# Loading q, k and v of an attention kernel into 128-partition tiles with longer rows

## The chip, the cores and the metric

The kernel runs on one core of a Trainium2 chip. The metric is the device time of one execution in microseconds. The core has five engines that the text names: TensorE (PE in the profile, its weight loads are PEld), VectorE (DVE), ScalarE (ACT), GpSimd (POOL) and SyncE (SP, which here issues all DMA transfers).

## The reference

The input has 4 batches, 8 heads, 576 tokens and head size 64. First a double attention: 32 learned rows p attend to k and v, and then q attends to the packed result. Two mixture-of-experts layers follow. Cut to the attention part:

```python
def sm_attn(qq, kk, vv):
    s = scale * np.matmul(qq, kk.transpose(0, 1, 3, 2))
    s = s - np.max(s, axis=-1, keepdims=True)
    a = np.exp(s)
    a = a / (np.sum(a, axis=-1, keepdims=True) + 1e-09)
    return np.matmul(a, vv)
p_packed = sm_attn(p, k, v)
out = sm_attn(q, p_packed, p_packed)
```

The output, as 2304 tokens of 512 features, goes through a first layer of 8 experts (each token to the expert with the largest logit, up to a capacity), and through a second with an output gate. Tensors are float32.

## The kernel before

**Attention.** A batch is worked in two halves G of four heads. Each half of k, q and v is one transfer into a tile "r" of 96 partitions: a partition holds, for each of the four heads, six tokens in sequence, 1536 contiguous bytes. `transp` turns k and q by TensorE transposes of [96, 128] into T (head size on partitions, the tokens' parity u in the upper and lower 64), and ScalarE evicts them from PSUM. `s1_mm` makes the first scores (p with k; the 32 rows p of four heads on 128 partitions), `s1_max` and `s1_exp` the first weights a1, `a1_T` transposes a1 back to tokens on partitions, and `pp_mm` multiplies by v. `pp_scale` and `pp_T` give the packed rows ppT.

The second softmax has only 32 columns. `s2_mm` makes its scores (q with ppT), `s2_tr` transposes them on VectorE in blocks of 32 by 32 into sT, where max, subtraction, exp, sum and product run over the 32 (the subtraction and the product on GpSimd), and `s2_back` transposes them back into a2T, whose columns are the tokens in order. For that, q's columns in T must have a certain order; the eviction of q writes them so, with a stride of three elements:

```python
if nm == "q":
    o = o.rearrange("x u (p j) -> x u j p", j=J)
    i = i.rearrange("x u (j p) -> x u j p", j=J)
```

**Order.** It is written out by hand. `att_iter(b)` does the first scores of batch b, the rest of batch b - 1, and the second softmax of batch b - 2, and transposes k of batch b + 1. Loads are issued on SP's queue ahead of each iteration: k of batch b + 2, then q's first half, v, and q's second half of batch b + 1. `att_last` does the last scores and the routing of batch 0, and `att_end` the rest, with pieces of the first expert layer filled in between. Logits of the gates (`g1_l`, from a2T) choose the experts whose weights SP then loads, so their place in time sets when the expert layers can start.

**Experts.** The weights are split into two float32r parts (`split`), and each product is made of three matmul passes. From the end of the attention on, TensorE runs the four expert layers nearly without a gap.

Of the kernel before, what the change touches and what calls it, by code (L numbers as in the profile page):

```python
# [28 lines left out]
def tile_kernel(  # L29
# [21 lines left out]
    KP = 96  # L51
    R = S // KP
    J = R // 2
    HS = S // 2
    NT = -(-S // 128)
# [44 lines left out]
    zt = const.tile([KP, 128], FP32, name="zt")  # L100
# [54 lines left out]
    # ================= gating: pieces =================  # L155
# [3 lines left out]
    def onehot(L, nm, V=nc.vector):  # L159
        """of the logits L [128,n,E]: bf16 one-hot of the first largest, and L less its largest; in two pieces"""  # L160
# [17 lines left out]
    def denom(ex, nm):  # L178
        """1 / (softmax sum + 1e-9)"""
        nc.scalar.activation(out=ex, in_=ex, func=ACTF.Exp)  # L180
        den = sm_p.tile([128, ex.shape[1]], FP32, tag=nm + "den", name="den")
        nc.vector.tensor_reduce(den, ex, axis=AX.X, op=ALU.add)
        nc.vector.tensor_scalar(den, den, 1e-9, None, op0=ALU.add)
        nc.vector.reciprocal(den, den)
        return den

    def counts(K16, dst):
        """dst [1,n,E] = kept tokens of each of n batches per expert"""
# [9 lines left out]
    def primary(c, nm, pe, mu, ne, V=nc.vector):  # L198
        """of the counts c [1,n,E]: the index of the largest, more than one?, any?"""
# [22 lines left out]
    # ================= attention =================  # L222
    att, att_r = ExitStack(), ExitStack()
    apool = pool_in(att)
    qkv_p = apool("qkv", 9)
# [24 lines left out]
    def load(b, nm, gs=(0, 1)):  # L250
        src = {"k": k, "q": q, "v": v}[nm]
        for G in gs:
            t = qkv_p.tile([KP, 4, R, D], FP32, tag="r", name="r")
            nc.sync.dma_start(t, src[b, 4 * G:4 * G + 4].rearrange("h (p r) d -> p h r d", r=R))
            raws[nm, b, G] = t

    def transp(b, nm, G, eng=0):
        """[96, 4 heads, row, d] -> [128 (row parity, d), 4 heads, 288]"""
        src = raws.pop((nm, b, G))
        t = t_p.tile([128, 4, HS], FP32, tag="T", name="T")  # L260
        for hh in range(2):
            ps = psm("tp")
            for u in range(2):
                for j in range(J):
                    tr(nc, ps[:, u, j * KP:(j + 1) * KP], src[:, 2 * hh + u, 2 * j:2 * j + 2, :].rearrange("p r d -> p (r d)"),
                       ident[:KP, :KP])
            i = ps[:, :, 0:HS]
            o = t[:, 2 * hh:2 * hh + 2, :]
            if nm == "q":
                o = o.rearrange("x u (p j) -> x u j p", j=J)  # L270
                i = i.rearrange("x u (j p) -> x u j p", j=J)
            evac(eng, o, i)
        T[nm, b, G] = t
# [9 lines left out]
    def score(lhs, rhs):  # L283
        """lhs(u, hq) [64,32], rhs [128, 4, 288] -> psum [128 (hq, pack), u, 288]"""
        s = psm("s")
        for hq in range(4):
            for u in range(2):
                mm(nc, s[32 * hq:32 * hq + 32, u, 0:HS], lhs(u, hq), rhs[64 * u:64 * u + 64, hq, :], True, True)
        return s
# [10 lines left out]
    def s1_exp(b, G):  # L300
        a1 = at_p.tile([128, 2, HS], FP32, tag="a1", name="a1")
        if G == 0:
            at["sm", b] = as_p.tile([128, 2], FP32, tag="sm", name="sm")
        nc.scalar.activation(out=a1, in_=at.pop(("s1", b, G))[:, :, 0:HS], func=ACTF.Exp,
# [8 lines left out]
    def a1_T(b, G, eng=0):  # L313
        a1 = at.pop(("a1", b, G))
        ps = psm("a1Tp")
        for u in range(2):
            for j in range(J):
                tr(nc, ps[:KP, u, j * 128:(j + 1) * 128], a1[:, u, j * KP:(j + 1) * KP], ident)
        t = at_p.tile([KP, 2, J, 128], FP32, tag="a1T", name="a1T")
        evac(eng, t, ps[:KP, :, 0:J * 128].rearrange("p u (j n) -> p u j n", j=J))  # L320
        at["a1T", b, G] = t

    def pp_mm(b, G):
        if G == 0:
            at["pp", b] = psm("pp")
        pp, t, vt = at["pp", b], at.pop(("a1T", b, G)), raws.pop(("v", b, G))
        for u in range(2):
            for j in range(J):
                for hq in range(4):
                    mm(nc, pp[32 * hq:32 * hq + 32, G, 0:D], t[:, u, j, 32 * hq:32 * hq + 32],  # L330
                       vt[:, hq, 2 * j + u, :], u == 0 and j == 0, u == 1 and j == J - 1)
# [52 lines left out]
    def s2_back(b, G):  # L384
        nc.vector.transpose(a2T[:, b, G].rearrange("p (n i u) -> p u n i", i=32, u=2), at.pop(("sT", b, G)))

# [11 lines left out]
    def g1_l(b0, b1):  # L398
        """logits' parts on partitions 32 (2 u + G) + E * place: of head group G, tokens 256 u .. 256 u + LW"""
# [29 lines left out]
    def gb(b0, b1):  # L429
        """rank of each token among the earlier ones of its expert"""  # L430
# [35 lines left out]
    # ================= experts =================  # L466
# [6 lines left out]
    def split(src, nm, i, lo_eng):  # L473
        """piece i of a weight matrix: two float32r parts that add up to it"""
# [12 lines left out]
    def new_h(last_first=False):  # L487
        """[128, chunk, token], high and low parts; last_first: the low parts of the last tile's tokens come first"""
# [3 lines left out]
    def moe1_load1(e):  # L492
        """the raw pieces of w1, rows split by head group: [128 (G, d), hq, f]"""
# [30 lines left out]
    def ppw_mm(pt, w):  # L524
        """(a2 pp) w1 = a2 (pp w1): pp w1 of 256 columns"""
# [15 lines left out]
    def chain(ps, seq, mid={}):  # L541
        """ps [128, 2, HS] = sum of stationary.T @ moving over seq; mid: other work, by the step it goes before"""
# [6 lines left out]
    def layer1(h, f, w, x, n, last_first=False):  # L549
        """h[f] = relu(w.T x), split; w, x: (hi, lo)"""  # L550
# [13 lines left out]
    def moe1_layer2(h, ws, c, y, mid={}):  # L564
        """y[c] = w2.T h, split"""
# [12 lines left out]
    def g2_l(y):  # L578
        """logits of both gates: rows from the high part of the gates, rows from the low part"""
# [28 lines left out]
    def g2_g(oel, g1s, slot):  # L608
        """the gates of the second experts, times those of the first"""
# [32 lines left out]
    def moe2_layer2(h, ws, t, g2, bsel):  # L642
        """rows of token tile t: (h.T w2) times the gates"""
# [62 lines left out]
    # ================= what the two slots leave =================  # L706
    def more(dst):
        """dst [1,1] = the number of batches and slots whose tokens go to more than one expert"""
# [4 lines left out]
    def slot(i, slots_i):  # L713
        """both expert layers of one more batch"""
# [24 lines left out]
    def general():  # L739
        """every expert over the tokens it is given, whatever the routing"""  # L740
# [25 lines left out]
        def mask(K):  # L766
            """msk [128, BT] = tokens of the loop's expert"""
# [5 lines left out]
        def masked(dst, src, b):  # L773
            """dst = src [128, n, S] where the expert's tokens are, else 0"""
# [76 lines left out]
    # ================= the program =================  # L851
# [5 lines left out]
    with tc.manual_schedule():  # L857
# [8 lines left out]
        def att_iter(b):  # L866
            """scores and weights 1 of batch b, the rest of batch b - 1, softmax 2 and logits of batch b - 2"""
# [46 lines left out]
        def att_last():  # L914
            """the last scores 1, with the gating of batch 0 between them"""
# [41 lines left out]
        def att_end():  # L957
            """the rest of the last batch"""
# [73 lines left out]
        # first expert layer of slot 0, between the pieces of the last batch  # L1032
# [82 lines left out]
        for i in (2, 3):  # L1115
            bz = val(slots_i[0:1, 0, i - 1:i], B - 1)
            nc.sync.dma_start(
                out.rearrange("(b p r) (x d) -> b p (r x) d", b=B, r=R, d=128)[bass.ds(bz, 1)].rearrange(
                    "o p r d -> p (o r) d"),
                zt.unsqueeze(1).to_broadcast([KP, S * DM // (KP * 128), 128]))  # L1120
# [90 lines left out]
```

## Time and profile before

| | us |
|---|---|
| median of 3 runs | 290.41 (287.1 to 293.39) |
| profiled execution: span from first to last instruction | 289.3 |
| TensorE busy | 259.8 (90%) |
| VectorE busy | 131.1 (45%) |
| ScalarE busy | 105.4 (36%) |
| GpSimd busy | 44.6 (15%) |
| DMA | 37.16 MB, 128 GB/s on average |

Of the profiled execution's own time the profile gives the span; it is 1.1 us below the median. Busy shares are means over stages with different limits, so the stages have to be looked at one by one. A row of a timeline or of a group names line, engine, operation, output tile, input tiles and the shape, partitions by elements; "[3.75 <-DMA r]" is idle time of the engine ahead of the instruction and what ended it. The DMA share is that of 16 engines, as a fraction; values a little above 1 occur where packets overlap.

### The profile page before, as it was taken

The page shows a single profiled execution, that of the slowest core. Times are in us where ns is not written, and L with a number is a line of the kernel's source. Part 1 is how long each engine was busy: PE and PEld are TensorE (multiplying, and loading weights), DVE is VectorE, ACT ScalarE, POOL GpSimd, SP SyncE. Part 2 cuts the span into 40 slices and gives each one's busy share as a digit, 9 for nine tenths or more (in the row PEclk, how much of TensorE's full clock was granted, in tenths as well). Part 3 has the DMA queues.
Part 4 walks back from the last instruction along what each step waited for, and adds up shares of the span by engine and source line. Part 5 has one row for each costly group of instructions (what it writes and reads, how often), then busy time and mean ns, then how long its engine had stood idle before and what let it go on. Part 6 is the DMA issues. An engine that isn't in the chain of part 4 may idle for free. (4 is left out here: it accounts for less than half of the span.)

```text
span 289.3 us, 5848 instructions
## 1 busy us (share of the span) xinstructions
PE 259.8 (90%) x2401; PEld 226.1 (78%) x2401; DVE 131.1 (45%) x316; ACT 105.4 (36%) x160; POOL 44.6 (15%) x69
## 2 busy tenths in 40 slices
PE   7785949969699898999979999999999999999990
PEld 5565739546479877997879999999888899998870
DVE  0230543858779948617972133359422053640000
ACT  2583537466435412125641224116232143431000
POOL 5000113315415206000533000000010000000100
PEclk9996975998889999999979999999999999999997
DMA  7999999990794000299378622502701181000111
GB/s 176 234 245 199 220 230 239 237 230 9 173 254 160 0 2 0 98 215 227 98 210 227 228 75 72 147 0 76 217 36 54 39 268 61 2 0 36 59 39 44
DMA packets 33828, 37.16 MB, mean 128 GB/s; under 512 B 4224, under 2 KB 30464, under 8 KB 33792
## 3 DMA queue, kind: packets, MB, share of 16 engines
q1 hardware_dynamic: 33792, 36.69, 50.2%
q8 instruction: 21, 0.34, 0.5%
q14 instruction: 15, 0.12, 0.1%
HBM read 31.25 MB, written 4.72 MB: 124 GB/s over the span
## 5 line engine op out<-in xcount | busy, mean ns | idle before, releaser
L21 PE MATMUL o<-w2bh,h 128*128 128x512 f32 x144 | 45.9, 391 | 0.0
L21 PE MATMUL y<-h,w2ah 128*128 128x288 f32 x256 | 44.6, 296 | 0.0
L21 PEld LDWEIGHTS y<-h,w2ah 128*128 128x128 f32 x256 | 37.6, 189 | 0.0
L562 DVE SCALAR_TENSOR_TENSOR h<-h 128x576 fp32r<-128x576 f32 (+3 forms) x64 | 25.8, 446 | 23.6 <-ACT h L555 23.6
L555 ACT ACTIVATE h<-h 128x576 fp32r<-128x576 f32 x32 | 20.4, 650 | 35.0 <-PE h L21 31.2
L25 PE MATMUL tp<-ident,r 96*128 96x96 f32 x192 | 24.1, 290 | 10.0 <-DMA r<-in_q_dram 8.0
L25 PEld LDWEIGHTS tp<-ident,r 96*128 96x128 f32 x192 | 21.8, 172 | 13.5 <-issue 11.0
L21 PEld LDWEIGHTS o<-w2bh,h 128*128 128x128 f32 x144 | 26.9, 188 | 5.7
L21 PE MATMUL o<-w2bl,h 128*128 128x512 f32 x80 | 31.3, 391 | 0.0
L236 ACT ACTIVATE T<-tp 128x576 f32<-128x576 f32 x32 | 24.0, 805 | 19.4 <-PE tp L25 19.2
L21 PE MATMUL y<-h,w2al 128*128 128x288 f32 x128 | 27.6, 297 | 0.7 <-DVE w2al L480 0.7
L21 PE MATMUL h<-yh,w1bh 128*128 128x288 f32 x128 | 27.5, 296 | 0.0
L21 PE MATMUL h<-yh,w1bl 128*128 128x288 f32 x128 | 27.4, 295 | 0.0
L21 PE MATMUL h<-yl,w1bh 128*128 128x288 f32 x128 | 27.3, 295 | 0.0
L21 PEld LDWEIGHTS y<-h,w2al 128*128 128x128 f32 x128 | 20.5, 188 | 1.5 <-DVE w2al L480 1.0
L480 POOL TENSOR_TENSOR w2al<-wraw,w2ah 128x1024 fp32r<-128x1024 f32 x6 | 14.2, 2392 | 44.1 <-DMA wraw<-in_moe_w_dram 26.3
L21 PEld LDWEIGHTS h<-yh,w1bh 128*128 128x128 f32 x128 | 20.6, 189 | 0.2
L21 PEld LDWEIGHTS h<-yh,w1bl 128*128 128x128 f32 x128 | 20.6, 188 | 0.0
L21 PEld LDWEIGHTS h<-yl,w1bh 128*128 128x128 f32 x128 | 20.6, 188 | 0.0
L661 POOL TENSOR_SCALAR osb<-osb,g 64x512 f32<-64x512 f32 x2 | 3.1, 1572 | 110.8 <-DVE osb L660 110.8
L571 ACT ACTIVATE yh<-y 128x576 fp32r<-128x576 f32 x8 | 5.2, 652 | 40.6 <-PE y L21 40.6
L653 ACT ACTIVATE osb<-o,g 128x512 f32<-128x512 f32 x8 | 5.5, 691 | 36.8 <-PE o L21 24.2
(173 smaller groups left out, 387.0 us busy)
## 6 DMA issues: line engine op xcount, KB each, us to landing
wraw<-in_moe_w_dram SPq DMA_DIRECT2D x24, 512.0 KB, 4.8
r<-in_k_dram SPq DMA_DIRECT2D x8, 576.0 KB, 12.4
r<-in_q_dram SPq DMA_DIRECT2D x8, 576.0 KB, 16.4
r<-in_v_dram SPq DMA_DIRECT2D x8, 576.0 KB, 16.4
wraw<-in_moe_w_dram SPq DMA_DIRECT2D x16, 256.0 KB, 5.4
out_dram<-zt SPq DMA_DIRECT2D x2, 1152.0 KB, 7.6
out_dram<-osb SPq DMA_DIRECT2D x8, 256.0 KB, 2.1
a2s<-a2T SPq DMA_DIRECT2D x1, 576.0 KB, 4.9
```

The lines of the kernel that those rows point to most:

```text
L21: return nc.tensor.matmul(out, lhsT=lhsT, rhs=rhs, start=start, stop=stop)
L25: return nc.tensor.transpose(out, in_, ident)
L236: nc.scalar.activation(out=o, in_=i, func=ACTF.Copy)
L480: lo_eng.tensor_tensor(lo, s, hi.bitcast(FP32), op=ALU.subtract)
L555: nc.scalar.activation(out=hi, in_=ps[:, :, 0:HS], func=ACTF.Relu)
L562: nc.vector.scalar_tensor_tensor(o, i, 0.0, a.bitcast(FP32), op0=ALU.max, op1=ALU.subtract)
L571: nc.scalar.activation(out=half(y[0][:, c, :]), in_=ps[:, :, 0:HS], func=ACTF.Copy)
L653: nc.scalar.activation(out=o[:n], in_=ps[:n, 0, :], func=ACTF.Copy, scale=g2[:n, t:t + 1])
L661: nc.gpsimd.tensor_scalar(o[:n], o[:n], g2[:n, t:t + 1], None, op0=ALU.mult)
```

## The change

Each half of q and k is loaded as 128 partitions (four heads by 32), a partition holding 18 tokens in sequence, 4608 contiguous bytes. v is loaded as 128 partitions by four heads by four tokens (1024 bytes), which covers 512 of the 576 tokens, and the last 64 tokens of all eight heads come in a third transfer of 64 partitions and 256-byte rows ("vr"). The pool of nine tiles becomes seven for q and k, four for v and two for vr. A half of q or k takes nine transposes of [128, 128], evicted as six and three, in the same way for q and k. The scores read their moving operand as nine pieces of 32 columns. The exp of the first softmax writes a1 in token order, with a stride of 18 elements; the a1 transposes read every fourth column (four transposes) and the last 64 columns (a fifth); their eviction becomes two instructions, and pp_mm has five steps instead of six. The transpose back into a2T writes with a stride of 18 elements instead of two. Comments that fell away are not shown, nor the renaming of KP to ZP for the tile of zeros.

```diff
-    KP = 96
-    R = S // KP
+    ZP = 96
+    TP = 32
+    R = S // TP
     J = R // 2
     HS = S // 2
+    VR = S // 128
+    VL = S - 128 * VR
...
-    qkv_p = apool("qkv", 9)
+    qk_p = apool("qk", 7)
+    v_p = apool("v", 4)
+    vr_p = apool("vr", 2)
     t_p = apool("t", 4)
...
     def load(b, nm, gs=(0, 1)):
+
         src = {"k": k, "q": q, "v": v}[nm]
         for G in gs:
-            t = qkv_p.tile([KP, 4, R, D], FP32, tag="r", name="r")
-            nc.sync.dma_start(t, src[b, 4 * G:4 * G + 4].rearrange("h (p r) d -> p h r d", r=R))
+            hs = slice(4 * G, 4 * G + 4)
+            if nm == "v":
+                t = v_p.tile([128, 4, VR, D], FP32, tag="v", name="v")
+                nc.sync.dma_start(t, src[b, hs, 0:128 * VR].rearrange("h (p r) d -> p h r d", r=VR))
+            else:
+                t = qk_p.tile([128, R, D], FP32, tag="r", name="r")
+                nc.sync.dma_start(t, src[b, hs].rearrange("h (p r) d -> (h p) r d", r=R))
             raws[nm, b, G] = t
+        if nm == "v":
+            t = vr_p.tile([VL, H, D], FP32, tag="vr", name="vr")
+            nc.sync.dma_start(t, src[b, :, 128 * VR:].rearrange("h p d -> p h d"))
+            raws["vr", b] = t
 
     def transp(b, nm, G, eng=0):
-        """[96, 4 heads, row, d] -> [128 (row parity, d), 4 heads, 288]"""
+
         src = raws.pop((nm, b, G))
-        t = t_p.tile([128, 4, HS], FP32, tag="T", name="T")
-        for hh in range(2):
+        t = t_p.tile([128, J, 128], FP32, tag="T", name="T")
+        for j0, n in ((0, 6), (6, 3)):
             ps = psm("tp")
-            for u in range(2):
-                for j in range(J):
-                    tr(nc, ps[:, u, j * KP:(j + 1) * KP], src[:, 2 * hh + u, 2 * j:2 * j + 2, :].rearrange("p r d -> p (r d)"),
-                       ident[:KP, :KP])
-            i = ps[:, :, 0:HS]
-            o = t[:, 2 * hh:2 * hh + 2, :]
-            if nm == "q":
-                o = o.rearrange("x u (p j) -> x u j p", j=J)
-                i = i.rearrange("x u (j p) -> x u j p", j=J)
-            evac(eng, o, i)
+            for j in range(n):
+                tr(nc, ps[:, j // 3, (j % 3) * 128:(j % 3) * 128 + 128],
+                   src[:, 2 * (j0 + j):2 * (j0 + j) + 2, :].rearrange("p r d -> p (r d)"), ident)
+            evac(eng, t[:, j0:j0 + n, :].rearrange("x (u j) c -> x u (j c)", j=3), ps[:, 0:n // 3, 0:384])
         T[nm, b, G] = t
...
     def score(lhs, rhs):
...
         for hq in range(4):
             for u in range(2):
-                mm(nc, s[32 * hq:32 * hq + 32, u, 0:HS], lhs(u, hq), rhs[64 * u:64 * u + 64, hq, :], True, True)
+                mm(nc, s[32 * hq:32 * hq + 32, u, 0:HS], lhs(u, hq),
+                   rhs[64 * u:64 * u + 64, :, TP * hq:TP * hq + TP], True, True)
         return s
...
     def s1_exp(b, G):
-        a1 = at_p.tile([128, 2, HS], FP32, tag="a1", name="a1")
+        a1 = at_p.tile([128, S], FP32, tag="a1", name="a1")
         if G == 0:
             at["sm", b] = as_p.tile([128, 2], FP32, tag="sm", name="sm")
-        nc.scalar.activation(out=a1, in_=at.pop(("s1", b, G))[:, :, 0:HS], func=ACTF.Exp,
+        nc.scalar.activation(out=a1.rearrange("p (i j u) -> p u j i", i=TP, u=2),
+                             in_=at.pop(("s1", b, G))[:, :, 0:HS].rearrange("p u (j i) -> p u j i", i=TP), func=ACTF.Exp,
                              bias=at.pop(("nb", b, G)), accum_out=at["sm", b][:, G:G + 1])
         at["a1", b, G] = a1
...
     def a1_T(b, G, eng=0):
         a1 = at.pop(("a1", b, G))
         ps = psm("a1Tp")
-        for u in range(2):
-            for j in range(J):
-                tr(nc, ps[:KP, u, j * 128:(j + 1) * 128], a1[:, u, j * KP:(j + 1) * KP], ident)
-        t = at_p.tile([KP, 2, J, 128], FP32, tag="a1T", name="a1T")
-        evac(eng, t, ps[:KP, :, 0:J * 128].rearrange("p u (j n) -> p u j n", j=J))
-        at["a1T", b, G] = t
+        for r in range(VR):
+            tr(nc, ps[:, r // 2, (r % 2) * 128:(r % 2) * 128 + 128], a1[:, r:128 * VR:VR], ident)
+        tr(nc, ps[:VL, 1, 256:384], a1[:, 128 * VR:], ident)
+        t = at_p.tile([128, VR, 128], FP32, tag="a1T", name="a1T")
+        tl = at_p.tile([VL, 128], FP32, tag="a1L", name="a1L")
+        evac(eng, t.rearrange("p (x r) n -> p x (r n)", x=2), ps[:, :, 0:256])
+        evac(eng, tl, ps[:VL, 1, 256:384])
+        at["a1T", b, G] = t, tl
 
     def pp_mm(b, G):
         if G == 0:
             at["pp", b] = psm("pp")
-        pp, t, vt = at["pp", b], at.pop(("a1T", b, G)), raws.pop(("v", b, G))
-        for u in range(2):
-            for j in range(J):
-                for hq in range(4):
-                    mm(nc, pp[32 * hq:32 * hq + 32, G, 0:D], t[:, u, j, 32 * hq:32 * hq + 32],
-                       vt[:, hq, 2 * j + u, :], u == 0 and j == 0, u == 1 and j == J - 1)
+        pp, (t, tl), vt, vr = at["pp", b], at.pop(("a1T", b, G)), raws.pop(("v", b, G)), raws["vr", b]
+        for r in range(VR + 1):
+            for hq in range(4):
+                hs = slice(32 * hq, 32 * hq + 32)
+                lhs, rhs = (t[:, r, hs], vt[:, hq, r, :]) if r < VR else (tl[:, hs], vr[:, 4 * G + hq, :])
+                mm(nc, pp[hs, G, 0:D], lhs, rhs, r == 0, r == VR)
...
     def s2_back(b, G):
-        nc.vector.transpose(a2T[:, b, G].rearrange("p (n i u) -> p u n i", i=32, u=2), at.pop(("sT", b, G)))
...
+        nc.vector.transpose(a2T[:, b, G].rearrange("p (i n u) -> p u n i", i=TP, u=2), at.pop(("sT", b, G)))
```

## Rows read from the trace of the kernel before

**Rows 1.** The page's 40 slices of 7.2 us: DMA share, rate.

```profile
DMA  7999999990794000299378622502701181000111
GB/s 176 234 245 199 220 230 239 237 230 9 173 254 160 0 2 0 98 215 227 98 210 227 228 75 72 147 0 76 217 36 54 39 268 61 2 0 36 59 39 44
```

**Rows 2.** Waits of TensorE: total us, times, longest us.

```profile
PE tp L25 <- DMA r<-in_q_dram: 8.0, 2, 4.3
...
PE pp L21 <- issue: 2.3, 1, 2.3
```

**Rows 3.** Windows by stage: busy us (and count) of each engine, clock, DMA share, GB/s.

```profile
0.00:17.04 17.04, 13.05 (x104) 9.56 (x105) 2.02 (x5) 7.42 (x14) 4.07 (x35) 1.00 0.96 211
17.04:33.83 16.79, 13.04 (x244) 10.54 (x242) 3.82 (x9) 9.47 (x16) 1.30 (x6) 0.80 1.04 217
33.83:54.41 20.58, 15.95 (x253) 12.31 (x248) 11.02 (x25) 9.65 (x16) 4.84 (x5) 0.75 1.09 234
54.41:68.16 13.75, 11.34 (x233) 7.83 (x230) 9.01 (x25) 9.15 (x14) 3.96 (x6) 0.88 0.82 184
68.16:84.50 16.34, 13.20 (x228) 9.85 (x220) 12.73 (x31) 7.38 (x10) 7.24 (x5) 0.90 0.69 143
84.50:104.40 19.90, 19.16 (x175) 15.58 (x173) 17.22 (x28) 8.59 (x13) 5.81 (x5) 1.00 0.31 98
```

**Rows 4.** Timeline of TensorE: start us, duration us, what, idle before it.

```profile
17.12 0.82 PE L25 MATMUL a1Tp<-ident,a 128*96 128x128 f32 x6
...
24.78 2.15 PE L25 MATMUL tp<-ident,r 96*128 96x96 f32 x12 [3.75 <-DMA r<-in_q_dram]
26.86 2.79 PE L21 MATMUL pp<-r,a1T 96*32 96x64 f32 x96
...
42.10 2.15 PE L25 MATMUL tp<-ident,r 96*128 96x96 f32 x12 [4.29 <-DMA r<-in_q_dram]
...
47.39 2.13 PE L25 MATMUL tp<-ident,r 96*128 96x96 f32 x12
...
55.20 0.72 PE L21 MATMUL s<-T,pT 64*32 64x288 f32 x16
...
56.23 1.16 PE L25 MATMUL tp<-ident,r 96*128 96x96 f32 x12
...
58.01 0.88 PE L21 MATMUL pp<-r,a1T 96*32 96x64 f32 x48
```

**Rows 5.** Windows with loads of different shapes.

```profile
42.00:62.00 20.00, 17.58 (x322) 13.73 (x323) 10.56 (x24) 11.48 (x20) 7.41 (x8) 0.78 1.08 238
84.20:88.20 4.00, 4.00 (x55) 3.25 (x54) 3.89 (x8) 1.90 (x3) 1.16 (x1) 1.00 1.04 319
120.20:123.00 2.80, 2.80 (x23) 2.80 (x22) 0.75 (x5) 0.45 (x1) 0.00 (x0) 1.00 0.67 254
145.00:148.00 3.00, 1.28 (x5) 1.31 (x6) 2.83 (x11) 0.00 (x0) 0.10 (x1) 0.71 0.96 260
232.20:238.00 5.80, 5.80 (x46) 5.80 (x45) 3.17 (x6) 2.65 (x4) 0.00 (x0) 1.00 0.90 287
```

**Rows 6.** Groups of ScalarE by form, 24 to 30 us.

```profile
L236 ACT ACTIVATE T<-tp 128x576 f32<-128x576 f32 x2 | 1.9, 950 | 4.3 <-PE tp L25 4.3
```

**Rows 7.** The same, 30.8 to 34.5 us.

```profile
L236 ACT ACTIVATE T<-tp 128x576 f32<-128x576 f32 x4 | 2.4, 648 | 0.2
```

**Rows 8.** Groups by form, the whole span.

```profile
L385 DVE STREAM_TRANSPOSE a2T<-sT 128x576 f32<-128x576 f32 x8 | 6.2, 769 | 0.4 <-POOL sT L382 0.4
...
L357 DVE STREAM_TRANSPOSE sT<-s 128x576 f32<-128x576 f32 x8 | 5.9, 762 | 0.4 <-PE s L21 0.3
...
L304 ACT ACTIVATE a<-s,nb 128x576 f32<-128x576 f32 x8 | 5.8, 724 | 1.9 <-DVE nb L297 1.4 <-DVE mx L163 0.5
...
L25 PEld LDWEIGHTS a1Tp<-ident,a 128*96 128x96 f32 x48 | 5.5, 134 | 1.2 <-issue 1.0 <-ACT T L236 0.2
```

**Rows 9.** Timeline of TensorE near 97 us.

```profile
97.57 0.53 PE L21 MATMUL y<-h,w2al 128*128 128x288 f32 x2 [0.74 <-DVE w2al L480]
```

More of the change, by code (lines that the diff above doesn't have):

```diff
@@ L99, in tile_kernel @@
         nc.gpsimd.memset(iob[:, b:b + 1], float(b))
-    zt = const.tile([KP, 128], FP32, name="zt")
+    zt = const.tile([ZP, 128], FP32, name="zt")
     nc.gpsimd.memset(zt, 0.0)
@@ L1117, in tile_kernel @@
             nc.sync.dma_start(
-                out.rearrange("(b p r) (x d) -> b p (r x) d", b=B, r=R, d=128)[bass.ds(bz, 1)].rearrange(
+                out.rearrange("(b p r) (x d) -> b p (r x) d", b=B, p=ZP, d=128)[bass.ds(bz, 1)].rearrange(
                     "o p r d -> p (o r) d"),
-                zt.unsqueeze(1).to_broadcast([KP, S * DM // (KP * 128), 128]))
+                zt.unsqueeze(1).to_broadcast([ZP, S * DM // (ZP * 128), 128]))
         e20 = val(e2_0[0:1, 0:1], E - 1)
```

## The prediction

> **What bounds the kernel now.** I read the 40 slices first [rows 1]. For the first 62 us or so the DMA engines are full and move some 235 GB/s; later they have gaps. So the loading of q, k and v may be a bound of its own at the front.
>
> TensorE's waits confirm it [rows 2]: its longest is for q, 8.0 us in two waits. I then cut the front into stages by the attention iterations [rows 3]: the opening (to 17.04), iteration 1 (16.79 us), iteration 2 (20.58 us), the last-scores stage (13.75 us), and two stretches in which the last batch and the first expert layer interleave (16.34 and 19.90 us); in the last of these TensorE is already busy 19.16 us, and from there on it sets the pace. The first three have a DMA share of about 1 or above; iterations 1 and 2 have clocks of 0.80 and 0.75. In the timeline both hold the same pattern: a wait for the second q transfer (3.75 and 4.29 us), then a stretch at the lower clock level, 1.2 GHz [rows 4]. The same 12 transposes take 2.15 us there and 1.16 us at 2.4 GHz. A late transfer is thus paid for twice.
>
> **The transfers.** Each q, k or v load is 0.590 MB, six per batch, 3.54 MB. The present shape (96 partitions, 1536-byte rows) moves 238 GB/s at share 1.08, that is 220 per unit of share [rows 5]; a batch needs about 15 us. Other stages show 128-partition loads: 1024-byte rows at 319 GB/s with share 1.04 (307), 2048-byte rows at 287 with 0.90 (319), and 4608-byte rows at 254 with 0.67 (379), though the last go from SBUF to SBUF [rows 5].
>
> The new q and k have 128 partitions and 4608-byte rows. I bound them by 319 and 379: four loads, 2.36 MB, in 6.2 to 7.4 us. The main v tile has 1024-byte rows, which are shorter than today's: 1.05 MB at 307 is 3.4 us. The v rest is 0.131 MB in 256-byte rows, which no row shows alone. The nearest is 512-byte rows at 260 GB/s [rows 5], so 0.5 us at that rate and 1.0 at half of it. A batch then needs 10.1 to 11.8 us, a mean of 11, about 4 less than now. Four batches then take 40 to 47 us of transfer instead of 60.
>
> The rest transfer is one more DMA per batch on SP's queue, ahead of the second q; that q gains more than the 0.5 to 1 us this costs it. The q/k loads get seven buffers and v four of its own, against nine shared, so a v load no longer waits for a freed q or k tile.
>
> **Where the time comes out.** Opening: the first two k transfers lie on the path; each saves 0.590 MB at 220 against 319 to 379, so 0.8 to 1.1 us, and the small p transfers queued behind them come sooner too. I take 2.0 of 1 to 3.
>
> Iteration 1: the wait of 3.75 goes; then, at 2.4 GHz, the 12 transposes save 0.99 (2.15 against 1.16), the 96 pp matmuls 1.03 (2.79 against twice 0.88) [rows 4]. That is 5.8, and I take 5.5, because ScalarE is busy 9.47 us of what would be 11 [rows 3], and it evicts in order. Iteration 2: 4.29 goes, the same 2.0 is saved, and its clock of 0.75 against 0.80 covers two k transposes more (the first 2.13, so another 0.97; the second mixed, about 0.5) [rows 4]: 7.8, of which I take 7.5. VectorE's 11.02 us then fill most of the 13 that are left.
>
> Last-scores stage: it has a stop of 2.3 us that is not put down to data ("issue") [rows 2] and a clock of 0.88; the DMA was still running. I take 1.0 of 0 to 2.3. **Gain: 2.0 + 5.5 + 7.5 + 1.0 = 16.0 us.**
>
> **The arithmetic changes.** Transposes of q and k go from 12 of 96 columns to 9 of 128, 1152 either way; six of 128 columns took 0.82 [rows 4], so nine take about 1.2. No change, at either clock. The a1 transposes go from 6 to 5 and the pp matmuls from 24 to 20 per half batch, 0.1 to 0.2 us saved each half, which I count as nothing. Scores read 9 pieces of 32 columns instead of 288 in a line; no row shows that, and I put it between 0 and half of one 0.72 us group [rows 4]: with 16 groups 0 to 5.8, taking 0, since each piece is itself contiguous.
>
> Evictions: a k eviction of 576 elements takes 648 ns [rows 7], one of q, written with a stride of 12 bytes, 950 ns [rows 6]. The new q is written straight: 16 times 0.3, 4.8 us less on ScalarE. But the stride moves to the exp of the first softmax, now 724 ns [rows 8], which will write every 72 bytes. One q eviction pays 0.3; with no two elements close together I allow 0.3 to 0.6: 8 times that, 2.4 to 4.8 us more. On ScalarE the two nearly cancel. The a1 eviction becomes two instructions, 0.1 us more each.
>
> The transpose back into a2T (VectorE) goes from a stride of 8 bytes to 72. Today it takes 769 ns against 762 for the unstrided one [rows 8], so 8 bytes are free; I take for 72 bytes the bounds 0 to 0.6. Six of the eight lie after 68 us, where VectorE is the crowded engine: 12.73 of 16.34 and 17.22 of 19.90 us [rows 3]. There TensorE already waits 0.74 us for a weight split behind them [rows 9], and the logits that choose the next experts follow the last two. Up to 3.6 us lost, and I take 2.0.
>
> The a1 transposes also read their stationary operand at a stride of 16 bytes. A load takes 134 ns today [rows 8] beside matmuls of about the same length. If it doubles, 4 loads in 8 calls expose 32 times 134 ns = 4.3 us. I take 1.0, as part of it lies beside matmuls.
>
> What is said of strides elsewhere: the Trainium skill (SBUF — State Buffer, Door 1: The DMA port swizzle) says that SBUF has 16-byte lines, wants two hits in each, and lets fp32 stride up to 4 elements for free. The trace agrees on 8 bytes and not on 12, which cost 302 ns here. By the page's stride limit the 16-byte stationary reads would cost nothing and the sum would be 1.0 better.
>
> **Sum.** 16.0 - 2.0 - 1.0 = 13.0 us saved from the profiled span of 289.3, so 276.3. The profiled execution's own time beyond its span is not shown; the median of the runs is 1.1 above the span, so I forecast 277.
>
> **Rivals.** (1) The engines take over sooner: with data early, the in-order queues of ScalarE and VectorE hold iterations 1 and 2 near 14.5 us each. They then fall from 37.4 to 29, the opening still saves 2.0, the last-scores stage nothing, and the late transposes cost their full 3.6: 8.4 + 2.0 - 3.6 = 6.8, so 283.6. For it speaks ScalarE's 9.47 us of in-order work; against it that TensorE runs iteration 1's first 4 us (to 24.78 less the wait of 3.75) without a stop today [rows 3, 4]. (2) Less is lost than I allow: strides cost nothing that shows, the 2.3 us stop goes whole (1.3 more than I take), and the iterations give their full 5.8 and 7.8 (0.6 more): 17.9, so 272.5. (3) It does not do what it says: rows from HBM stay at 220 per unit of share whatever their length. Then only v gains (4.2 MB at 307 against 220, 5.4 us, less the rest's 2 to 4), and the strides' 3.0 take it back: 290. Against it speak the 1024- and 2048-byte rows. (4) Slower: the scattered write of the back transposes. Its six late ones lie on a VectorE with 6.3 us of slack in two stretches [rows 3]. The rest of the change gives 15 (16.0 less 1.0); so it decides once the six add 21 us, 3.6 each, nearly five times their present 0.77. At eight times (5.4 more each, 32 - 6.3 - 15) the kernel loses 11: 301. Nothing at 12 bytes hints at such a price.
>
> **How the numbers follow.** Forecast 0.55, rival (1) 0.17, (2) 0.17, (3) 0.06, (4) 0.05. What a measurement can tell from no change is about 2 percent, so 284.6 and below counts as faster: the forecast, rival (2), and three fifths of (1), 0.82. Same: the rest of (1) and (3), 0.13. Slower 0.05. The range takes in (2) and (1) with the unknown stride costs: 269 to 285.
>
> **What would show it.** After the change the DMA share should fall below 1 well before 60 us; no long wait of TensorE for q should be left in iterations 1 and 2, and the granted clock there should be near 1. The last-scores stage should end near 52 to 53 us instead of 68.16. Exp should take 1.0 to 1.3 us, the back transposes up to 1.4. If iterations stay above 14 us with ScalarE or VectorE full, rival (1) holds; if DMA share is still full at 60 us, rival (3). What would make me wrong above all is a strided access that costs several times what 12 bytes cost.

## The result, and the profile after

The changed kernel takes 275.2 us (median of four runs, 274.9 to 278.8) against 291.1 us for the kernel before in the same comparison; the ratio is 0.956, with a 95% interval from 0.944 to 0.968. The profiled execution took 275.5 us with a span of 273.4, so about 2 us lie around the span. Its span is 15.9 us shorter than that of before.

The 40 slices of the page (6.8 us each) answer to [rows 1]:

```profile
DMA  7999997049720004973878224008302270001111
GB/s 233 375 301 300 380 326 217 2 109 217 218 77 2 0 0 153 225 195 94 234 195 285 79 77 156 0 3 234 112 19 77 83 267 2 0 0 42 59 41 47
```

The front load is over in the seventh slice, at about 45 us, instead of about 62; from the second slice to the sixth it moves 300 to 380 GB/s instead of some 235. TensorE's waits (total us, times, longest us) answer to [rows 2]:

```profile
PE tp L25 <- DMA r<-in_q_dram: 3.2, 2, 2.1
```

The 8.0 us for q have become 3.2, not nothing: 1.05 are left in iteration 1 and 2.14 in iteration 2. The stop of 2.3 us that was put down to "issue" does not occur. The same stages as in [rows 3], cut at the same instructions (busy us and count of each engine, clock, DMA share, GB/s):

```profile
0.00:13.05 13.05, 10.12 (x92) 7.31 (x93) 2.02 (x5) 7.73 (x14) 4.06 (x35) 1.00 0.88 303
13.05:24.64 11.59, 10.54 (x212) 7.75 (x210) 3.75 (x10) 9.40 (x18) 1.30 (x6) 1.00 1.06 303
24.64:41.48 16.84, 13.47 (x223) 9.03 (x218) 11.79 (x26) 9.24 (x17) 4.84 (x5) 0.90 1.06 343
41.48:51.90 10.42, 9.71 (x208) 6.85 (x205) 8.74 (x26) 8.53 (x16) 3.27 (x5) 1.00 0.47 127
51.90:68.90 17.00, 13.15 (x205) 9.53 (x197) 14.12 (x31) 6.58 (x12) 7.89 (x6) 0.90 0.68 141
```

The opening is 4.0 us shorter, iteration 1 5.2, iteration 2 3.7, the last-scores stage 3.3: 16.3 us in all. The next stretch is 0.7 us longer, and the one after it, up to where the second expert product resumes (89.72 instead of 104.38), about 0.9. That leaves 14.7; the last 1.2 come later.

TensorE's timeline shows the opening and what is left of the two waits (start us, duration us, what, idle before it):

```profile
4.85 1.17 PE L25 MATMUL tp<-ident,r 128*128 128x128 f32 x9 [0.31 <-DMA r<-in_k_dram]
...
15.42 0.75 PE L25 MATMUL a1Tp<-ident,a 128*128 128x128 f32 x5
...
17.93 1.17 PE L25 MATMUL tp<-ident,r 128*128 128x128 f32 x9 [1.05 <-DMA r<-in_q_dram]
19.03 0.65 PE L21 MATMUL pp<-v,a1T 128*32 128x64 f32 x32
19.61 0.32 PE L21 MATMUL pp<-vr,a1L 64*32 64x64 f32 x8
...
30.77 1.44 PE L25 MATMUL tp<-ident,r 128*128 128x128 f32 x9 [2.14 <-DMA r<-in_q_dram]
32.13 1.08 PE L21 MATMUL pp<-v,a1T 128*32 128x64 f32 x32
33.15 0.44 PE L21 MATMUL pp<-vr,a1L 64*32 64x64 f32 x8
...
82.71 0.53 PE L21 MATMUL y<-h,w2al 128*128 128x288 f32 x2 [0.93 <-DVE w2al L493]
```

The first nine transposes already run at the upper clock level, and data come 0.9 us sooner than in the kernel before, where the transposes started at 5.73. In two more executions of the changed kernel the first nine took 2.04 and 2.09 us, nearly the 2.15 of 1.2 GHz, and only the second nine 1.15 and 1.17. In iteration 2 the old pattern is still there, smaller: a wait for q's second half, then work at 1.2 GHz. Groups by form (mean ns of one behind the busy time) answer to [rows 6 to 8]:

```profile
L241 ACT ACTIVATE T<-tp 128x768 f32<-128x768 f32 x16 | 13.0, 810 | 9.6 <-PE tp L25 9.6
L314 ACT ACTIVATE a<-s,nb 128x576 f32<-128x576 f32 x8 | 10.6, 1341 | 0.9 <-DVE nb L307 0.6 <-DVE mx L166 0.3
L398 DVE STREAM_TRANSPOSE a2T<-sT 128x576 f32<-128x576 f32 x8 | 9.9, 1244 | 0.0
...
L25 PEld LDWEIGHTS tp<-ident,r 128*128 128x128 f32 x144 | 15.9, 142 | 6.9 <-issue 2.6 <-ACT a L314 1.6 <-POOL lgT L153 0.6
L25 PEld LDWEIGHTS a1Tp<-ident,a 128*128 128x128 f32 x32 | 4.5, 207 | 1.5 <-ACT T L241 0.9 <-issue 0.5
```

Exp went from 724 to 1341 ns, the transpose back from 769 to 1244. Two weight loads of 128 columns stand side by side here: 142 ns from contiguous columns, 207 from columns 16 bytes apart.

### The profile page after: what moved, and what is told of

Its sections match the earlier page's. It is cut to its first block, busy times and chain, and to the rows that moved or that the text cites. A ratio compares the mean times of both kernels' runs of the same rounds, so it can differ in the third digit from the quotient of the medians.

```text
span 273.4 us, 5623 instructions
## 1 busy us (share of the span) xinstructions
PE 249.4 (91%) x2281; PEld 215.3 (79%) x2281; DVE 134.4 (49%) x319; ACT 103.9 (38%) x165; POOL 44.5 (16%) x69
## 4 chain that ended last, share of the span: by engine, by line
PE 70%; DVE 14%; DMA 10%; SPq 2%; issue 1%; ACT 1%; POOL 0%; ACTq 0%; DVEq 0%; POOLq 0%
PE h L21 23%; PE o L21 19%; PE y L21 18%; DMA r<-in_q_dram 6%; PE tp L25 2%; PE pp L21 2%; DMA wraw<-in_moe_w_dram 2%; DVE eq L208 2%; DVE a2T L398 2%; PE lp L21 2%; PE l L21 2%; DVE h L575 2%; DMA r<-in_k_dram 1%; DVE dn L389 1%; SPq L269 1%; PE ppw L21 1%
## 5 line engine op out<-in xcount | busy, mean ns | idle before, releaser
L241 ACT ACTIVATE T<-tp 128x768 f32<-128x768 f32 (+1 forms) x32 | 18.9, 648 | 9.6 <-PE tp L25 9.6
L25 PE MATMUL tp<-ident,r 128*128 128x128 f32 x144 | 18.8, 278 | 3.8 <-DMA r<-in_q_dram 3.2
L21 PEld LDWEIGHTS y<-h,w2al 128*128 128x128 f32 x128 | 20.5, 188 | 1.7 <-DVE w2al L493 1.2
L25 PEld LDWEIGHTS tp<-ident,r 128*128 128x128 f32 x144 | 15.9, 142 | 6.9 <-issue 2.6
L21 PEld LDWEIGHTS h<-yh,w1bh 128*128 128x128 f32 x128 | 20.6, 189 | 0.2
L21 PEld LDWEIGHTS h<-yh,w1bl 128*128 128x128 f32 x128 | 20.6, 188 | 0.0
L21 PEld LDWEIGHTS h<-yl,w1bh 128*128 128x128 f32 x128 | 20.6, 188 | 0.0
## 6 DMA issues: line engine op xcount, KB each, us to landing
v<-in_v_dram SPq DMA_DIRECT2D x8, 512.0 KB, 10.4
```

What stands on the lines that cost most here:

```text
L21: return nc.tensor.matmul(out, lhsT=lhsT, rhs=rhs, start=start, stop=stop)
L25: return nc.tensor.transpose(out, in_, ident)
L241: nc.scalar.activation(out=o, in_=i, func=ACTF.Copy)
```

## The experiments

Each ratio is to the kernel before, measured beside it, with its 95% interval; each diff is against the changed kernel unless it says otherwise, and "..." marks what is left out of it. The changed kernel itself, measured twice more, gave 0.953 (0.946 to 0.960) and 0.956 (0.949 to 0.963), that is 276.9 and 277.6 us. Its 16 executions lie between 273.9 and 279.1 us, so two medians that differ by 2 us are not clearly apart. The theory at the outset was the prediction's: the transfers are what gains, and the strides take some of it back. The rivals were that the arithmetic or the order of work gains (fewer instructions, q's straight eviction, the buffers), and that the length of the rows is what makes the transfers fast.

**The two parts alone.** The first keeps the new q and k and loads v as before, with six a1 transposes of 96 columns at a stride of 24 bytes; the second keeps the new v and loads q and k as before.

```diff
 e1_newqk_oldv
...
-                t = v_p.tile([128, 4, VR, D], FP32, tag="v", name="v")
+                t = v_p.tile([96, 4, 6, D], FP32, tag="v", name="v")
...
 e2_oldqk_newv
...
-                t = qk_p.tile([128, R, D], FP32, tag="r", name="r")
+                t = qk_p.tile([96, 4, 6, D], FP32, tag="r", name="r")
...
```

> q and k as in the changed kernel, v as before (96 partitions, 1536-byte rows), the a1 transposes six of 96 columns read with a stride of six. If the arrival of the data sets the front (my theory), a batch's transfers take 2.36 MB at about 360 GB/s and 1.18 MB at 220, about 12 us against 10.4 in the changed kernel and 15 before: most of the gain stays, TensorE's waits for q grow by 1 to 4 us, time 277 to 281. If the gain is mostly the shorter arithmetic of the transposes and evictions (rival), the time is that of the changed kernel, 275 to 276. If v's new shape gave it, 287 or more.

> v as in the changed kernel, q and k as before (96 partitions, 1536-byte rows, their transposes, scores, the strided eviction of q and the transposition back as before); six q and k tiles instead of seven, for room. My theory: a batch still needs 2.36 MB at 220 GB/s and 1.18 MB at 300, about 14.5 us, so little is gained: 285 to 290, the two waits for q near their 3.75 and 4.29 us. If v's rest transfer and its order in the queue, not q and k, made the difference: 278 to 282.

The first took 281.5 us, ratio 0.964 (0.952 to 0.977); the second 285.95, ratio 0.982 (0.972 to 0.991). With v of old the waits for q add up to 2.7 us, with q and k of old to 5.3. Windows of 12 to 20 us:

```profile
12.00:20.00 8.00, 5.50 (x66) 4.26 (x66) 2.54 (x4) 5.26 (x9) 0.30 (x1) 0.96 1.06 314
```

(new q and k, old v), and

```profile
12.00:20.00 8.00, 7.12 (x92) 5.21 (x80) 2.52 (x5) 6.45 (x13) 0.29 (x1) 1.00 1.12 272
```

(old q and k, new v). The rates stand between 235 and the changed kernel's. Each part gains by itself, and the part with four of the six tiles gains about twice as much (10.5 us against 5.3, by the ratios). In both, the waits came out otherwise than expected. With q and k of old they are 3.15 and 2.12 us, below the old 3.75 and 4.29. With v of old they did not grow against the changed kernel's 3.2 us; what is lost there lies mostly in the last-scores stage (15.6 us against 10.4), which holds a stop that the profile puts down to no data:

```profile
54.17 0.20 PE L21 MATMUL rk<-oh,ones 128*128 128x16 bf16 x2 [3.59 <-issue]
```

The first run's interval also overlaps the changed kernel's. So what v's shape adds as a transfer is not shown.

**Row length against partitions.** q and k on 128 partitions, but in rows of 1536 bytes as before, with gaps of 64 bytes between them in SBUF.

```diff
-                t = qk_p.tile([128, R, D], FP32, tag="r", name="r")
-                nc.sync.dma_start(t, src[b, hs].rearrange("h (p r) d -> (h p) r d", r=R))
+                t = qk_p.tile([128, 3, 6 * D + 16], FP32, tag="r", name="r")
+                nc.sync.dma_start(t[:, :, 0:6 * D], src[b, hs].rearrange("h (p c r) d -> (h p) c (r d)", c=3, r=6))
...
```

> The changed kernel, but each q and k partition is written in three pieces of 1536 bytes with a gap of 64 bytes between them, so that the transfer has 128 partitions and the old row length. If the 128 partitions make the rate, q and k still move at 300 GB/s or more in DMA windows and the time is 275 to 279. If the row length makes it, the rate in the first 40 us falls to some 220 to 240 GB/s, the waits for q come back at about 3 to 4 us each, and the time is 285 to 290.

It took 279.2 us beside 292.2 for the kernel before: ratio 0.955 (0.946 to 0.965), as the changed kernel's. Windows of 4 to 44 us, of the kernel before, this run and the changed kernel in turn, then a window of this run alone:

```profile
4.00:44.00 40.00, 29.09 (x400) 22.55 (x398) 10.94 (x22) 18.95 (x34) 3.81 (x12) 0.87 1.07 226
4.00:44.00 40.00, 34.55 (x498) 25.41 (x498) 14.40 (x36) 25.23 (x46) 6.09 (x14) 0.91 1.01 300
4.00:44.00 40.00, 33.78 (x539) 23.87 (x538) 19.17 (x44) 26.27 (x49) 8.14 (x15) 0.96 1.06 334
...
32.00:40.00 8.00, 4.99 (x90) 4.00 (x91) 1.86 (x5) 3.50 (x8) 3.68 (x4) 0.64 1.08 359
```

Per unit of share, the 40 us give 211, 297 and 315 GB/s. In its best window this run reaches 332 (359 at 1.08, q's rows mixed with v's), where rows of 1536 bytes gave 220 on 96 partitions [rows 5]. So the number of partitions makes most of the rate, and the 4608-byte rows add little that the time shows. They may not be worth nothing: the wait for q in iteration 2 is longer here than the 2.1 to 2.7 us of the changed kernel's three traces.

```profile
35.01 2.15 PE L25 MATMUL tp<-ident,r 128*128 128x128 f32 x9 [3.71 <-DMA r<-in_q_dram]
```

A rule in the Trainium skill (SBUF — State Buffer, Door 1: The DMA port swizzle) fits: bandwidth depends on how many of the 16 ports a tile's partitions reach, and by its formula the partitions 0 to 95 fill eight ports and half fill the other eight. By that page the same time per full port would give three quarters of the rate, as an estimate; the runs show 211 against 297 over the 40 us (0.71) and 220 against 332 in the windows (0.66).

**The transfer time put back.** Behind each half of q and k, 13 of its 18 tokens per partition are loaded once more into a tile that nothing reads. A batch then moves 5.25 MB, about 15 us at 350 GB/s, as long as a batch took in before. All the new arithmetic stays.

```diff
...
+                dump = dump_p.tile([128, 13, D], FP32, tag="dump", name="dump")
+                nc.sync.dma_start(dump, src[b, hs].rearrange("h (p r) d -> (h p) r d", r=R)[:, 0:13])
```

> The changed kernel with 13 of every 18 rows of each q and k half loaded a second time into a tile that nobody reads (1.7 MB more per batch). Nothing of the arithmetic changes. My theory: a batch's transfers take about 15 us again, the waits for q in iterations 1 and 2 come back (over 3 us each) with a lowered clock behind them, and the time is 285 to 291. The rival, that the arithmetic gave the gain: 275 to 278.

It took 287.8 us, ratio 0.985 (0.976 to 0.994). The long wait of iteration 2 is back, with the low clock behind it:

```profile
15.39 0.44 PE L25 MATMUL pTp<-ident,p_sb 128*128 128x128 f32 x2 [3.18 <-POOL p_sb L254]
...
24.02 1.17 PE L25 MATMUL tp<-ident,r 128*128 128x128 f32 x9 [1.01 <-DMA r<-in_q_dram]
...
41.20 2.15 PE L25 MATMUL tp<-ident,r 128*128 128x128 f32 x9 [5.09 <-DMA r<-in_q_dram]
```

Of the changed kernel's gain, 13 us (0.045 of 292), about 4.3 are left. By this run some two thirds of the gain is transfer time, and the arithmetic and the order of work account for the other third. The split is rough, since the old load did not come back exactly: iteration 1's wait is 1.01 us, not over 3, iteration 2's is longer than before (5.09 against 4.29), and the opening ends at 18.4 us instead of 17.0. Less these 1.4 us, transfer time is still more than half of the gain, as an estimate.

**The stride of the transposes back.** The write of a2T goes back to a stride of 8 bytes; the order of the tokens in a2T, and so of the rows of the output, is then another.

```diff
-        nc.vector.transpose(a2T[:, b, G].rearrange("p (i n u) -> p u n i", i=TP, u=2), at.pop(("sT", b, G)))
+        nc.vector.transpose(a2T[:, b, G].rearrange("p (n i u) -> p u n i", i=32, u=2), at.pop(("sT", b, G)))
```

> The changed kernel, but the transposition back into a2T writes with a stride of two elements as it did before, so the tokens of a batch stand in another order in a2T and in the output. Each of the eight instructions should go from 1.24 back to 0.77 us. If VectorE sets the pace after 52 us, where six of them lie, the time falls by 1.5 to 3 us against the changed kernel (273). If the instructions lie beside TensorE's work, as the unchanged distance from the first expert pieces to the logits suggests, it stays within 1 us.

It took 275.0 us beside 276.9 of the changed kernel, ratios 0.950 (0.944 to 0.957) and 0.953 (0.946 to 0.960): the medians differ by 1.9 us, the intervals overlap. Its transposes back:

```profile
L398 DVE STREAM_TRANSPOSE a2T<-sT 128x576 f32<-128x576 f32 x8 | 6.1, 767 | 0.4 <-POOL sT L395 0.4
```

TensorE's first expert matmuls (h), its wait for the weight split (y) and the logits (lp):

```profile
65.27 0.53 PE L21 MATMUL h<-xh,wh 128*128 128x288 f32 x2
...
81.62 0.53 PE L21 MATMUL y<-h,w2al 128*128 128x288 f32 x2 [0.74 <-DVE w2al L493]
...
85.01 3.51 PE L21 MATMUL lp<-a2T,gsz 128*32 128x320 f32 x24
```

In the changed kernel's profiled execution the same two points are these:

```profile
65.49 0.60 PE L21 MATMUL h<-xh,wh 128*128 128x288 f32 x2
...
86.09 3.71 PE L21 MATMUL lp<-a2T,gsz 128*32 128x320 f32 x24
```

With the write at 8 bytes the wait for the weight split is that of before [rows 9], 0.74 us against 0.93. From the first expert matmul to the logits it takes 19.7 us with it and 20.6 in the changed kernel (19.9 before, so the distance was not unchanged, as the expectation has it). Over all traces it takes 19.7 to 20.1 us in the four with the write at 8 bytes, and 20.5 to 21.9 in the ten with the write at 72: the scattered write puts the logits off by some 1.2 us on average. The total does not show it by itself: the run with fewer buffers (below) has the scattered write and took 274.9 us.

**No stride anywhere.** v in the layout of q and k, so that it needs no rest transfer; exp writes in a line, VectorE transposes a1 in blocks of 32 by 32, and pp takes 72 matmuls of 32 rows per half.

```diff
...
-        ps = psm("a1Tp")
-        for r in range(VR):
-            tr(nc, ps[:, r // 2, (r % 2) * 128:(r % 2) * 128 + 128], a1[:, r:128 * VR:VR], ident)
...
+        nc.vector.transpose(t, a1.rearrange("p u (j i) -> p u j i", i=32))
...
-                mm(nc, pp[hs, G, 0:D], lhs, rhs, r == 0, r == VR)
+                mm(nc, pp[hs, G, 0:D], t[hs, r % 2, r // 2, :], vt[hs, r, :], r == 0, r == R - 1)
```

> The changed kernel with v loaded in the layout of q and k too (128 partitions, 4608-byte rows, no rest transfer), exp written without a stride, and a1 transposed on VectorE in blocks of 32 by 32 instead of on TensorE; pp has 72 matmuls of 32 rows per half instead of 20. If what is left of the front is still the arrival of q in iteration 2 (2.1 us and the lower clock behind it), a batch's 3.54 MB at about 360 GB/s come in under 10 us, that wait goes, ScalarE loses 0.6 us per exp, and the time is 270 to 273. If VectorE's eight more transposes of 0.77 us (for three copies of 0.95) or the 52 more matmuls per half take it back: 275 to 278.

It took 293.4 us, ratio 1.014 (1.007 to 1.020): 1.4% slower than before, and outside both expected ranges. The wait for q is 0.64 us in iteration 1, and none is left in iteration 2; but:

```profile
17.18 3.09 PE L21 MATMUL pp<-v,a1T 32*32 32x64 f32 x204
23.25 2.56 PE L21 MATMUL pp<-v,a1T 32*32 32x64 f32 x84 [2.97 <-issue]
...
71.38 3.65 PE L21 MATMUL pp<-v,a1T 32*32 32x64 f32 x144 [4.69 <-DVE a1T L317]
```

288 small matmuls take the place of 80 ahead of the rest of the iteration (the trace counts each of them twice), and TensorE stands for 2.97 us among them without waiting for data; such stops in front of pp add up to 5.5 us, and in front of other work to 3.4. Later TensorE waits 4.69 us for VectorE's transposes of a1. What is saved on ScalarE and in waits for q is lost on TensorE and in waiting for VectorE.

**Buffers.** Six tiles for q and k instead of seven, three for v instead of four.

```diff
-    qk_p = apool("qk", 7)
-    v_p = apool("v", 4)
+    qk_p = apool("qk", 6)
+    v_p = apool("v", 3)
```

> The changed kernel with six q and k tiles and three v tiles instead of seven and four, nine in all as before. If the transfers' rate made the gain: within 1 us of the changed kernel. If the two more tiles made it, loads are held up on SP's queue by tiles not yet free, the waits for q in iterations 1 and 2 grow by over 2 us, and the time is 278 or more.

274.9 us, ratio 0.952 (0.944 to 0.959), with one wait for q, of 2.1 us: no slower than the 276.9 of the changed kernel beside it. The pools do not make the gain.

**What is left of the wait, ScalarE's room, and the opening's clock.** Three kernels ran beside the changed one.

> The changed kernel again, as the base for the other three of this call. Every theory: 275 to 277 us, ratio to the kernel before 0.950 to 0.958.

It took 277.6 us, ratio 0.956.

The kernel before with a longer warm-up (diff against the kernel before):

```diff
-        warm(16)
+        warm(22)
```

> The kernel before with 22 instead of 16 warm-up matmuls, nothing else. In the kernel before the warm-up ends 1.0 us ahead of the first k tile, and the opening then runs at 1.2 GHz (12 transposes in 2.15 us). Theory A (the idle gap between the warm-up and the first k transpose keeps the clock low, so part of the changed kernel's 4 us gain of the opening is the smaller gap): six more at 0.22 us each close the gap, the level rises before 8 us, the second k transposes take about 1.17 us, and the opening ends about 15 instead of 17.0 us. Theory B (the level in the opening is a matter of the execution, or of what follows): transposes still at 2.15 us, opening 17 us. Total in both: 288 to 292 us, as iteration 1 still waits for q, so that an earlier opening is mostly spent in that wait.

289.85 us, ratio 0.999 (0.994 to 1.004). Its timeline:

```profile
5.96 1.56 PE L25 MATMUL tp<-ident,r 96*128 96x96 f32 x12
...
8.88 1.18 PE L25 MATMUL tp<-ident,r 96*128 96x96 f32 x12 [1.13 <-DMA r<-in_k_dram]
...
14.27 0.44 PE L25 MATMUL pTp<-ident,p_sb 128*128 128x128 f32 x2 [2.20 <-POOL p_sb L248]
...
25.16 2.15 PE L25 MATMUL tp<-ident,r 96*128 96x96 f32 x12 [4.73 <-DMA r<-in_q_dram]
```

As theory A says, without the idle gap the level rises during the first transposes; the run has six more matmuls as well as no gap, and does not tell the two apart. But the opening ends at 16.53, only 0.6 sooner, since a wait of 2.20 us for p takes the place, and iteration 1 then waits 4.73 us for q instead of 3.75. A faster opening alone is worth nothing here, while the loads set the end of the iteration.

Both halves of q ahead of v, the constants behind them, 18 warm-up matmuls:

```diff
-        warm(16)
+        warm(18)
...
-        load(0, "q", (0,))
+        load(0, "q")
         load(0, "v")
-        load(0, "q", (1,))
...
+            if b + 1 < B:
+                load(b + 1, "q")
+                load(b + 1, "v")
             if b == 0:
                 load_consts()
-            if b + 1 < B:
-                load(b + 1, "q", (0,))
-                load(b + 1, "v")
-                load(b + 1, "q", (1,))
```

> The changed kernel with both halves of q loaded ahead of v, the loads of the small constants behind them instead of ahead, and 18 warm-up matmuls instead of 16. Theory A (what is left of iteration 2's wait comes from the place of q's second half on SP's queue: it is issued at 22.7 us, behind the constants and v): it is issued by about 15 us, the 2.1 us wait for q at 30.8 goes, with the low clock behind it (2 to 3 us), and the kernel takes 272 to 274 us. Rival B (the DMA engines are full to that point, so that any order delivers the last byte at the same time): the wait moves from q to v or its rest, about 2 us in front of the pp matmuls, and the kernel takes 275 to 277 us, the same as the changed one.

280.0 us, ratio 0.966 (0.960 to 0.973): slower than the changed kernel, and neither theory's case. The constants hold the gate's weights, which the end of iteration 1 needs:

```profile
28.70 0.38 PE L21 MATMUL gp<-wg_sb,ppT 64*32 64x8 f32 x9 [5.50 <-DMA wg_sb<-in_moe_w_gate_dram]
```

Behind this wait no wait for q is left, but the wait itself has given the loads that time. Whether q ahead of v helps with the gate's weights left in front was not tried, so the theory stays open.

A further ScalarE instruction behind each exp:

```diff
+        jk = ab_p.tile([128, 512], BF16, tag="jk", name="jk")
+        nc.scalar.activation(out=jk, in_=a1[:, 0:512], func=ACTF.Copy)
```

> The changed kernel with one more ScalarE instruction behind every exp of the first softmax: a copy of 128x512 into a tile that nothing reads, about 0.6 to 0.7 us, eight times, 5 us in all: the price of the exp's stride (0.62 us) paid once more. Theory A (the stride of exp lies beside other work; the ScalarE queue has room): 275 to 277 us, no change that can be measured. Rival B (ScalarE's in-order queue sets the iterations): 5 us more, 280 to 281 us.

274.1 us, ratio 0.944 (0.938 to 0.951), 3.5 us below the changed kernel beside it, with intervals that just overlap. Groups by form and TensorE's timeline:

```profile
L319 ACT ACTIVATE jk<-a 128x512 bf16<-128x512 f32 x8 | 5.0, 630 | 0.3
```

```profile
30.68 1.17 PE L25 MATMUL tp<-ident,r 128*128 128x128 f32 x9 [0.92 <-ACT a L314]
```

The 5.0 us more of ScalarE cost nothing, so ScalarE's queue has room for exp's 0.62 us, which is as long. One thing the copy does not test: it stands behind exp, while a slower exp also makes a1 itself later. Why the kernel is not just as fast but faster is only in part seen: q's second half is there at 30.68, the short wait is one for ScalarE, and iteration 2 takes 15.3 us (25.84 to 41.17) instead of 17.5 (25.90 to 43.36) in the execution beside it, whose wait for q is 2.70 us. What made the load earlier is open.

## Why the prediction was right, and where its steps were off

The forecast of 277 us and its reason hold: the transfers gain, and the rest takes little back. The measured 275.2 lies between it and the 272.5 of rival (2). On the span 15.9 us were saved instead of 13.0; from the span to the time it is 2.1 us, where the forecast added 1.1. By the sum's steps:

- **Transfers: right.** A batch was put at 10.1 to 11.8 us; 3.54 MB at the 303 to 343 GB/s of the first three stages are 10.3 to 11.7. All of q, k and v was put at 40 to 47 us and is over at about 45. The rates that it took came from rows that differ from the old load in partitions and in length at once; which of the two makes the rate it did not say. Most of it is the partitions: 1536-byte rows on 128 of them give 297 per unit of share over 40 us. Rival (3) fell with the rate.
- **Opening: 4.0 instead of 2.0.** This term was mis-sized. The nearer 0.9 us came from the earlier transfer, as worked out. The step left out the clock: with the gap between warm-up and first data down from 1.01 to 0.31 us the transposes ran at 2.4 GHz (1.17 us) where before took 2.15 for each of two groups. That the gap does it is borne out by the longer warm-up in the kernel before and by the other traces (last section), but is not tested apart from the warm-up's length. It is not sure in each execution that the change closes it: the run with 1536-byte rows had a gap of 0.68 us and 2.15 again, and its opening ended at 16.4 us.
- **Iteration 1: 5.2 for 5.5.** The size and the clock of 1.00 are right, but the wait did not go whole: 1.05 us of the 3.75 stay.
- **Iteration 2: 3.7 for 7.5.** The step that failed is that the whole wait of 4.29 goes. 2.14 us of it stay, and the low level behind it costs 0.27 in the transposes and about 1.1 in the pp matmuls (twice 1.08 + 0.44 against 0.65 + 0.32): 3.5 of the missing 3.8. The transfers got faster, but iteration 1 shrank to 11.6 us, which is what a batch's transfer takes: the loads still set the pace there, at a DMA share of 1.06. Even the run without this wait (ScalarE's extra copy) has an iteration 2 of 15.3, a gain of 5.3, since short waits for ScalarE (0.92 us in one place) come next; the 7.5 was too much in any case.
- **Last-scores stage: 3.3 for 1.0.** The stop of 2.3 us went whole and the clock is 1.00, as in rival (2). Stops put down to "issue" of 0.9 us and more stand in the traces with 2401 and 2407 TensorE instructions (2.3 and 2.0 us), with 2353 (3.6), with 2329 (0.9) and with 3073 (up to 2.97), and in none with 2281 or 2283. That the shorter program removes it is likely from that row of cases, and not tested by itself.
- **Stationary reads at 16 bytes: 1.0 taken.** A load took 65 ns more (207 against 142 beside it, not against the 134 of 96 columns [rows 8]). Little of it shows: five transposes take 0.75 us (at 15.42 us, for one), where five ninths of the 1.17 of contiguous ones are 0.65; 0.1 us, eight times, is 0.8. The rule of the Trainium skill cited in the prediction (SBUF — State Buffer, Door 1: The DMA port swizzle), four fp32 elements for free, did not hold in the load itself.
- **Transposes back: 2.0 taken of 0 to 3.6.** 475 ns more each, inside the 0 to 0.6; the scattered write puts off the logits by some 1.2 us. Rival (4), a price of several times the 769 ns, fell. The two late stretches lost 1.6 us in all.
- **Exp: 1341 ns, just above the 1.0 to 1.3 that was expected.** The added copy shows that ScalarE's queue has room for it; so the cover named there, ScalarE's other work, is likely, and what a later a1 costs is not shown.
- **Rival (1)**, engines that take over at 14.5 us per iteration, fell in iteration 1 (11.59 us).

The stages' gains were 16.3 us, which hold nearly all of the price of the stationary reads; the sum has 16.0 less 1.0 for these. The late loss was 1.6 against 2.0. That the two sums come so close is luck in part: iteration 2's shortfall of 3.8 was made up by the opening and the last-scores stage (2.0 and 2.3 more). The last 1.2 us of the span were in no step, and they are luck too. Behind a wait of 2.4 us in an expert layer the kernel before ran at 1.2 GHz (clock 0.71 in [rows 5]); the changed kernel has the same wait, ran on at 2.4 GHz in its profiled execution, and in one of its two further traces at 1.2. Six pairs of matmuls take 3.00 us at the one level and 1.68 at the other. The kernel before, the changed one, and the other execution of it, in turn:

```profile
146.72 0.82 PE L21 MATMUL h<-xh,wh 128*128 128x288 f32 x2 [2.38 <-DVE h L562]
147.34 0.68 PE L21 MATMUL h<-xl,wh 128*128 128x288 f32 x2
...
132.04 0.50 PE L21 MATMUL h<-xh,wh 128*128 128x288 f32 x2 [2.39 <-DVE h L575]
132.38 0.42 PE L21 MATMUL h<-xl,wh 128*128 128x288 f32 x2
...
132.90 0.82 PE L21 MATMUL h<-xh,wh 128*128 128x288 f32 x2 [2.38 <-DVE h L575]
133.51 0.68 PE L21 MATMUL h<-xl,wh 128*128 128x288 f32 x2
```

## What to carry to other kernels

Before making rows longer, fill the partitions: over 40 us of loading, 1536-byte rows gave 211 GB/s per unit of share on 96 partitions, and 297 with q and k on 128. When a load is sped up, compare its time with the stage as it will be after the gain, not as it is; a wait goes only as far as the stage stays longer than the transfer. A strided write belongs where its engine has room: ScalarE had room for 0.6 us more in the loading stages, while 0.5 us more on VectorE beside the expert layers put off the logits.

## What was not expected of the hardware

- Writes at a stride of 72 bytes took 1.9 times (exp, 724 to 1341 ns) and 1.6 times (VectorE's transpose, 769 to 1244 ns) as long as with lines and with 8 bytes; 8 bytes were free (769 against 762 ns).
- A load of 128 stationary columns 16 bytes apart took 207 ns instead of 142.
- The opening's clock goes with the idle gap between the warm-up and the first k tile. In the eleven executions with a gap of 0 to 0.5 us the second k tile's transposes ran at 2.4 GHz (1.15 to 1.18 us for a tile), and a later gap of up to 1.8 us ahead of them did not lower the level; in the three with 0.68 to 1.01 us both tiles ran at 1.2 (2.15 us).
- Small matmuls (32 by 32, 64 columns) met stops of up to 2.97 us that no data explain.
